# Attention beside a Fourier filter on one core: every fourth part of the maxima takes the bank of the background products

## The chip, the cores and the metric

The kernel runs on one core of a Trainium2 chip. The metric is the device time of one execution in microseconds. A core has engines that run their own instruction streams and wait for one another by semaphores: TensorE (PE; its weight load is PEld), VectorE (DVE), ScalarE (ACT), GpSimd (POOL), and SyncE (SP), which here only issues transfers (DMAs). TensorE writes its products into PSUM, a memory of eight banks per partition; one bank holds 512 float32 values of each of 128 partitions. DVE and ACT read them from there.

## What is computed

Two independent parts, whose results stand side by side in the output:

```python
# A: attention with a compressive memory, 32 heads of 18, four segments of 512 rows
q, k, v = x @ wq, x @ wk, x @ wv            # per head and segment
for s in range(4):
    p = softmax(qs @ ks.T * scale + mask)   # causal inside the segment
    a_dot = p @ vs
    a_mem = (phi(qs) @ M) / (phi(qs) @ z + 1e-6)
    outs.append(g * a_mem + (1 - g) * a_dot)
    M += phi(ks).T @ vs;  z += phi(ks).sum()
a = concat(outs) @ wo
# B: a global filter
b = irfft2(rfft2(x) * (w_r + 1j * w_i))
```

## The kernel before

The program runs in three stretches: the forward transform of B with the projections of A; the inverse transform of B, into which the first steps of the attention are already woven (the prologue); and the attention itself, from about 347 us on, which this text is about. Its order is written out by hand: engines execute their instructions as the Python code emits them.

The attention loop (`attention`) runs over steps `t` from 0 to 132. A step is one head of one segment, 512 queries against 512 keys; four steps make a group `k` and eight steps a stack of eight heads. Segment `g` holds 32 steps. In one step four kinds of work are interleaved on PE:

- `s1(t+11)`, the **maxima**, eleven steps ahead. It computes the scores of a head once, in bf16, only to find the row maxima. Each `part` takes one PSUM bank, fills it with matmuls (line 687), and DVE reduces it with a custom instruction and a read of the accumulator (line 691). An even step of the loop has three parts (384 and 128 columns; 512; two of 256), an odd step two, so four steps have ten.
- `mpath`, once in four steps: the maxima of four heads are copied by POOL (lines 703, 704), transposed by PE into a bank (`mt`, line 707, also tag "s1"), copied by ACT (line 710) and sent by a DMA into two more rows of the queries, so that the next product has the maximum subtracted.
- `s2(t)`, the **scores again**, keys on the partitions, in banks of tag "s2" (lines 723, 727, 728, 733). ACT takes the exponential of each bank into `P` (lines 724, 729, 734), and POOL clears the triangle above the diagonal (line 736).
- `pv`, in every odd step sixteen matmuls of `P` with the values into bank "pv" (line 760); ACT copies the sum out once in four steps (`U`, line 766).

Beside them runs the **background** list `bg`: one piece of a generator is emitted in some of the steps by `run_bg(rate)`. It first holds `late_setup` (loads and casts of the output weights, no PSUM); from step 34 on `den` (denominators of the memory), and, appended by a lane that prepares reciprocals, `mixed` and `oproj` of the segment before (memory products, combination, output projection). Their products take tag "post" through `post(...)`, which turns to tag "s1" from step 117 on.

PSUM in the attention: `s1` has three banks (pool `ps1`), `s2` three, `pv` one and `post` one:

```python
ps1=L1.enter_context(PP(tc,"ps1",dict(s1=3)))
...
tp=pool(es,"tp2",2); ps=es.enter_context(PP(tc,"ps",dict(s2=3,pv=1,post=1)))
```

A tag's banks are taken in turn, so a new tile waits until the reader of the tile that had the bank is done; for `s1` that is the tile three back, where `mt` counts as one.

Of the kernel before, what the change touches and what calls it, by code (L numbers as in the profile page):

```python
# [5 lines left out]
F32=mybir.dt.float32; F32R=mybir.dt.float32r  # L6
# [403 lines left out]
class ATT:  # L410
# [268 lines left out]
    def s1(s,t):  # L679

        nc=s.nc; k,hh=divmod(t,4); n,qd=divmod(k,2); h=4*qd+hh
        Q,K=s.Qs[n%3],s.Ks[n%4]; tp=s.sm
        assert (n,0) in s.loaded and (n,1) in s.loaded,(t,n)
        if hh==0: s.mg[k]=tp.tile([128,4,4],F32,name="mg")
        def part(*J):
            p=s.ps1.tile([128,512],F32,name="s1",tag="s1")
            for o,i,e in J: nc.tensor.matmul(p[:,o:o+128*i+128],Q[:108,h+e,128*i:128*i+128],K[:108,h+e,:128*(i+1)],start=True,stop=True)  # L687
            for o,i,e in J:
                w=128*(i+1); b=max(256,w-128*e)
                junk=tp.tile([128,b],BF,name=f"junk{b}",bufs=1)  # L690
                nc.vector.tensor_tensor_reduce(out=junk[:,:w],in0=p[:,o:o+w],in1=s.mask[:,512-w:],scale=1.0,scalar=-3.0e38,  # L691
                    op0=OP.add,op1=OP.max,accum_out=s.mg[k][:,hh+e,i:i+1])
        part((0,2,0),(384,0,0))
        yield
        part((0,3,0))
        yield
        if hh%2: part((0,1,-1),(256,1,0))
        yield
# [247 lines left out]
    def begin(s,sm,sp,ps1):  # L946
        s.late=[]; s.now=-1
        s.sm,s.sp,s.ps1=sm,sp,ps1
        s.mh=sm.tile([128,8,16],BF,name="mh",bufs=1); s.nc.gpsimd.memset(s.mh,0.0)
        s.mg={};s.P={};s.vs={};s.rc={};s.am={};s.pq={};s.ux={};s.rate=1.2;s.potag=s.rest=None  # L950
    def prologue(s):

        nc,io=s.nc,s.io
        yield
        s.load_v(0)
        q=s.stack_dmas(1,0)+s.stack_dmas(1,1)+s.stack_dmas(2,0)+s.stack_dmas(2,1)+[lambda: s.load_v(1)]+s.stack_dmas(3,1)
        for i in range(2): yield
        i=0
        for t in range(11):
            for _ in s.s1(t):  # L960
                for _ in range(1+(i%24==0)):
                    if q: q.pop(0)()
                i+=1
                yield
            if 2<=t<6: nc.gpsimd.dma_start(s.Ks[t-2][108:110].rearrange("p h c -> p (h c)"),io["neg1"])
            if t in (3,7): m=s.mpath(t//4); next(m)
            if t in (4,8): next(m); next(m,None)
        assert not q
# [3 lines left out]
    def attention(s,tp,ps):  # L972
        nc=s.nc; s.tp,s.ps,s.psm,s.mtag=tp,ps,s.ps1,"s1"
        s.homes()
        def steps(gen,i):
            for _ in range(i):
                try: next(gen)
                except StopIteration: return
        m=None
        q=[]  # L980
        qu=[]
        bg=[s.late_setup(tp)]
        state=dict(acc=0.0)
        def run_bg(rate):
            state["acc"]+=rate
            if state["acc"]>=1:
                state["acc"]-=1
                while bg:
                    try: next(bg[0]); break
                    except StopIteration: bg.pop(0)  # L990
        lane=[]
        for t in range(133):
            k,hh=divmod(t,4); n,qd=divmod(k,2); g=k//8
            if hh==0 and qd==0:
                if 0<n<14: q+=s.stack_dmas(n+2,0)
                if 0<n<13: q+=s.stack_dmas(n+3,1)
                if n+2<16: q.insert(6,lambda n=n: s.load_v(n+2))
            st=t%32
            if t in (18,21,24,27,30): s.pq_load(1,ORD[(18,21,24,27,30).index(t)])
            if t==34: bg.append(s.den(1,lane))  # L1000
            if st==8 and g>0:
                def ln(g=g):
                    r=s.recip(s.rD[g-1],s.rrD[g-1],s.g1,False,"rr",2)
                    for i in range(8):
                        if 2<i<6: s.ux_load(g-1,ORD[i-3])
                        next(r); yield
                    yield from r
                    bg.append(s.mixed(g))
                    o=s.oproj(g-1)
                    if g<3: bg.append(itertools.islice(o,4)); bg.append(s.den(g+1,lane))  # L1010
                    bg.append(o)
                lane.append(ln())
            if t==125: lane.append(s.recip(s.rD[3],s.rrD[3],s.g1,False,"rr"))
            a=s.s1(t+11) if t+11<128 else iter(())
            b=s.s2(t) if t<128 else iter(())
            for _ in range(3 if t%8==0 else 1):
                if q: q.pop(0)()
            if qu: qu.pop(0)()
            steps(a,1)
            steps(b,1)  # L1020
            run_bg(0)
            steps(a,1)
            steps(b,1)
            if 4<=t-1<132: s.pv((t-5)//4,(t-5)%4)
            run_bg(s.rate)
            steps(a,1)
            if hh==1 and m is not None: steps(m,1)
            steps(b,1)
            if hh==1 and m is not None: steps(m,1)
            if hh==0 and k+2<32: m=s.mpath(k+2); next(m)  # L1030
            if hh==0 and s.rest: s.rest(); s.rest=None
            if t>=7 and t%4==3:
                s.pv_out((t-7)//4)
                if t%8==3:
                    u=s.u_dmas((t-11)//8)
                    if t<124: s.later(1,lambda u=u: qu.extend(u))
                    else: qu+=u
            for l in list(lane):
                try: next(l)
                except StopIteration: lane.remove(l)  # L1040
            if qu: qu.pop(0)()
            s.due(t)
        assert not q
        s.potag="s2"; s.last_parts()
        if qu: qu.pop(0)()
        b=s.recip(s.rD[3],s.rrD[0],s.g1,False,"rd"); next(b)
        for u in range(3): s.ux_load(3,u)
        while qu: qu.pop(0)()
        i=0
        while bg or i<10:  # L1050
            for l in list(lane):
                try: next(l)
                except StopIteration: lane.remove(l)
            run_bg(1.0)
            i+=1
            s.due(132+i)
            if i in (3,8,10): s.last_tile((3,8,10).index(i),"rr")
            if i==3: s.ux_load(3,3)
            if i==5: next(b); next(b); next(b)
            if i in (6,7): next(b)  # L1060
            if i==7: s.ux_load(3,4)
        assert not lane
        s.due(999)
        for _ in b: pass
        s.last_low()
        for t in range(3):
            for u in range(7):
                s.last_proj(u,t)
                if t==2 and u==3: s.last_low()
                if t==2 and u in (1,4): s.last_tile(3 if u==1 else 4,"rd")  # L1070
        s.last_low()
        for u in range(7): s.last_proj(u,3)
        o=[s.tp.tile([128,4,512],F32,name=f"P{i}").rearrange("p a b -> p (a b)") for i in range(2)]
        o=[o[tb//3][:,576*(tb%3):576*(tb%3)+576] for tb in range(4)]
        nc=s.nc
        for u in range(8):
            if u==6:
                for t in range(4): s.last_proj(7,t)
            tb,hf=divmod(u,2); s.last_proj(u,4); c=slice(288*hf,288*hf+288) if u>5 else slice(0,576)
            (nc.vector.tensor_copy if hf else nc.scalar.copy)(o[tb][:,288*hf:288*hf+288],s.acc[u])  # L1080
            if hf or u>5: nc.sync.dma_start(s.io["ya"][1536+128*tb:1664+128*tb,c],o[tb][:,c])
# [108 lines left out]
```

## Time and profile before

| | |
|---|---|
| runs shown | 683.86, 684.14, 684.6 us (median 684.14) |
| profiled execution | 683.95 us; span from first to last instruction 682.2 us |
| busy share of the span | PE 98%, weight load 71%, DVE 79%, ACT 64%, POOL 28% |
| granted TensorE clock | 0.999 |
| costliest groups in the attention | maxima on DVE (line 691) 219.6 us, pv on PE (line 760) 82.2 us |

In the profile a row is one instruction or a run of like ones: start, length, engine, line, operation, tiles. A number in brackets at the end of a row is the engine's idle time just before it, and what ended that idle time. "idle" counts only time with no instruction recorded as running; PE's matmuls are pipelined, so the next one may start well before the row of the last one ends.

### The profile page before, as it was taken

How to read it: one execution, taken by the hardware profiler on the slowest of the kernel's cores; microseconds unless marked ns; L12 is line 12 of the kernel's file. 1: busy time of each engine (PE TensorE's matmuls, PEld its weight loads, DVE VectorE, ACT ScalarE, POOL GpSimd, SP SyncE). 2: the span in 40 equal slices, each digit the busy share in tenths (PEclk: the TensorE clock that was granted, in tenths of full speed). 3: DMA queues.
4: the chain of work that ended last, by engine and by line, in shares of the span. 5: the costliest groups of instructions: out<-in, count | busy, mean ns of one | idle time of the engine just before them, and what ended most of it. 6: DMA issues, size and time to landing. Idle time of an engine off the chain costs nothing.

```text
span 682.2 us, 14101 instructions
## 1 busy us (share of the span) xinstructions
PE 669.0 (98%) x4776; PEld 487.0 (71%) x4776; DVE 541.0 (79%) x1509; ACT 433.5 (64%) x900; POOL 193.0 (28%) x392
## 2 busy tenths in 40 slices
PE   9999999999999999999989999999999999999997
PEld 5999779879879879999954444444566445663497
DVE  5998989889789779598778888998766888667543
ACT  4876795585585384544358877777756777656521
POOL 2111000100200102556416433445323663135410
PEclk9999999999999999999999999999999999999999
DMA  9896476596387679699336765776646576423152
GB/s 338 301 311 186 137 198 200 151 300 203 113 240 222 178 211 319 196 284 272 110 121 176 207 185 151 204 205 174 173 139 188 155 186 167 125 87 92 29 170 78
DMA packets 76034, 127.57 MB, mean 187 GB/s; under 512 B 12813, under 2 KB 44203, under 8 KB 72371
## 3 DMA queue, kind: packets, MB, share of 16 engines
q1 hardware_dynamic: 69310, 110.67, 55.7%
q0 software_dynamic: 5632, 15.76, 8.0%
q8 instruction: 37, 0.61, 0.4%
q10 hardware_dynamic: 1020, 0.25, 0.2%
q14 instruction: 35, 0.28, 0.1%
HBM read 81.78 MB, written 43.92 MB: 184 GB/s over the span
## 4 chain that ended last, share of the span: by engine, by line
PE 84%; DVE 5%; DMA 4%; ACT 3%; issue 2%; POOL 1%; SPq 0%; ACTq 0%; DVEq 0%; POOLq 0%
PE pj L487 15%; PE pv L760 11%; PE s L687 11%; PE pjv L487 8%; PE po L908 5%; PE i L331 4%; PE i L320 4%; PE f L145 4%; PE c L166 4%; PE s L723 3%; PE s L727 3%; PE pn L835 2%; PE s L733 2%; PE po L937 2%; PE pm L559 2%
## 5 line engine op out<-in xcount | busy, mean ns | idle before, releaser
L691 DVE CUSTOM_DVE_ANT_0 junk<-s,x 128x384 bf16<-128x384 f32 (+3 forms) x512 | 219.6, 486 | 49.0 <-PE s L687 47.6
L736 POOL TENSOR_SCALAR_AFFINE_SELECT P<-P 128x512 f32<-128x512 f32 (+2 forms) x135 | 80.3, 617 | 61.3 <-ACT P L724 58.0
L760 PE MATMUL pv<-P,vs 128*32 128x512 f32 (+3 forms) x1024 | 82.2, 439 | 0.5 <-POOL P L736 0.4
L724 ACT ACTIVATE P<-s 128x512 f32<-128x512 f32 x128 | 77.3, 604 | 8.3 <-PE s L723 7.1
L729 ACT ACTIVATE P<-s 128x512 f32<-128x512 f32 x128 | 77.0, 602 | 2.8 <-PE s L728 2.7
L734 ACT ACTIVATE P<-s 128x512 f32<-128x512 f32 x64 | 38.3, 598 | 46.3 <-PE s L733 45.4
L687 PE MATMUL s<-Ks,Qs 108*128 108x512 bf16 (+3 forms) x256 | 57.9, 299 | 2.2 <-DVE mg L691 2.0
L760 PEld LDWEIGHTS pv<-P,vs 128*32 128x32 f32 x1024 | 26.8, 109 | 45.5 <-issue 36.3
L487 PE MATMUL pj<-x,wqkh 128*128 128x512 f32 x162 | 56.1, 408 | 0.0
L232 DVE TENSOR_TENSOR Z<-Z 128x580 f32<-128x580 f32 (+2 forms) x51 | 45.9, 913 | 0.6
L691 DVE DVE_READ_ACCUMULATOR2_ANT mg<- 128x1 f32 x512 | 42.5, 83 | 0.0
L548 POOL MEMSET vt<- 128x32 f32 x16 | 2.3, 162 | 139.2 <-PE pm L559 79.2
L320 PE MATMUL i<-civ,Y 128*128 128x256 f32 (+1 forms) x288 | 39.6, 289 | 0.9 <-POOL Y L305 0.9
L687 PEld LDWEIGHTS <-Qs 108*128 108x128 bf16 x320 | 29.5, 97 | 13.0 <-issue 6.2
L320 PEld LDWEIGHTS i<-civ,Y 128*128 128x128 f32 (+1 forms) x288 | 36.8, 181 | 1.9 <-POOL Y L305 1.3
L331 PE MATMUL i<-itab,T 128*128 128x290 f32 (+1 forms) x224 | 36.0, 304 | 0.1
L487 PE MATMUL pj<-x,wqkl 128*128 128x512 f32 x90 | 35.5, 395 | 0.0
L487 PE MATMUL pj<-xh,wqkh 128*128 128x512 f32 x90 | 35.5, 395 | 0.0
L487 PE MATMUL pj<-xh,wqkl 128*128 128x512 f32 x90 | 35.5, 395 | 0.0
L487 PEld LDWEIGHTS pj<-x,wqkh 128*128 128x128 f32 x162 | 30.5, 189 | 6.4
L506 DVE SCALAR_TENSOR_TENSOR ex<-pj,ex 128x512 f32<-128x512 f32 (+1 forms) x28 | 19.3, 689 | 19.4 <-ACT ex L504 19.4
L500 ACT CAST sp<-pj 128x512 bf16<-128x512 f32 x36 | 21.3, 591 | 18.1 <-PE pj L487 14.4
(207 smaller groups left out, 1697.2 us busy)
## 6 DMA issues: line engine op xcount, KB each, us to landing
qkD<-sp SPq DMA_DIRECT2D x32, 384.0 KB
xin<-xb SPq DMA_DIRECT2D x16, 384.0 KB
cfw<-cfw POOLq DMA_DIRECT2D x16, 384.0 KB, 5.1
civ<-civ POOLq DMA_DIRECT2D x16, 384.0 KB, 7.7
Ks<-qkD SPq DMA_DIRECT2D x12, 512.0 KB
x<-qkD SPq DMA_DIRECT2D x10, 512.0 KB
Qs<-qkD SPq DMA_DIRECT2D x10, 512.0 KB
vs<-vD SPq DMA_DIRECT2D x16, 310.5 KB
```

Of the source, the lines that this page charges most:

```text
L232: s.nc.vector.tensor_tensor(o,a,b,op=op)
L320: nc.tensor.matmul(p[:m,k],Y[i][:,q,c*128:c*128+m],cc[:,hl,o:o+256],start=n==0,stop=n==5)
L331: nc.tensor.matmul(p,x,t,start=n==0,stop=n==6)
L487: s.nc.tensor.matmul(out,a,b,start=i==0,stop=i==len(L)-1)
L687: for o,i,e in J: nc.tensor.matmul(p[:,o:o+128*i+128],Q[:108,h+e,128*i:128*i+128],K[:108,h+e,:128*(i+1)],start=True,stop=True)
L691: nc.vector.tensor_tensor_reduce(out=junk[:,:w],in0=p[:,o:o+w],in1=s.mask[:,512-w:],scale=1.0,scalar=-3.0e38, op0=OP.add,op1=OP.max,accum_ ...
L724: nc.scalar.activation(P[0][:,hh],p0,AF.Exp,scale=SC)
L729: nc.scalar.activation(P[1][:,hh],p1,AF.Exp,scale=SC)
L734: nc.scalar.activation(P[2][:,hh-1:hh+1].rearrange("p h c -> p (h c)"),p2,AF.Exp,scale=SC)
L736: nc.gpsimd.affine_select(out=x[:,a:b],in_=x[:,a:b],pattern=[[0,b-a],[1,128]],compare_op=OP.is_ge,fill=0.0,base=0,channel_multiplier=-1)
L760: nc.tensor.matmul(s.pvt[32*hh:32*hh+32,128*j:],vt[:,152*j+19*h:152*j+19*h+32],mv[0][:,hh,mv[1]],start=j==0,stop=j>1,skip_group_check=True)
L908: nc.tensor.matmul(ps,a[t][:r,c],b[:r,t,w],start=i==0,stop=i==13)
```

## The change

A counter `n1` counts the parts of the maxima. While a flag `spare` is set, every fourth part takes its bank from tag "post" instead of "s1". The flag is set at the top of each step: before step 34, and later whenever the background list is empty at that moment. It is not set in the prologue.

```diff
         def part(*J):
-            p=s.ps1.tile([128,512],F32,name="s1",tag="s1")
+            s.n1+=1
+            p=s.ps.tile([128,512],F32,name="s1",tag="post") if s.spare and s.n1%4==0 else s.ps1.tile([128,512],F32,name="s1",tag="s1")
             for o,i,e in J: nc.tensor.matmul(p[:,o:o+128*i+128],Q[:108,h+e,128*i:128*i+128],K[:108,h+e,:128*(i+1)],start=True,stop=True)
...
-        s.mg={};s.P={};s.vs={};s.rc={};s.am={};s.pq={};s.ux={};s.rate=1.2;s.potag=s.rest=None
+        s.mg={};s.P={};s.vs={};s.rc={};s.am={};s.pq={};s.ux={};s.rate=1.2;s.potag=s.rest=None; s.n1=0; s.spare=False
...
         for t in range(133):
+            s.spare=t<34 or not bg
             k,hh=divmod(t,4); n,qd=divmod(k,2); g=k//8
```

The order of the instructions is the same on every engine; what differs is for which semaphore some of them wait. PE in steps 6 and 7 of the loop, before (`s_...` are score banks; those of line 687 are parts of the maxima, those of lines 723 to 728 the second scores):

```order
L687 LDWEIGHTS Qs_3168
L687 MATMUL s_4492<-Ks_3170,Qs_3168 128x512 [waits DVE_49]
L727 LDWEIGHTS x_2634
L727 MATMUL s_4496<-x_2634 128x384 [waits Activation_49]
L728 LDWEIGHTS x_2634
L728 MATMUL s_4496<-x_2634 128x128
L687 LDWEIGHTS Qs_3168 [waits PE_49]
L687 MATMUL s_4502<-Ks_3170,Qs_3168 128x256 [waits Activation_49]
L687 LDWEIGHTS Qs_3168
L687 MATMUL s_4502<-Ks_3170,Qs_3168 128x256
L687 LDWEIGHTS Qs_3168
L687 MATMUL s_4510<-Ks_3170,Qs_3168 128x384 [waits DVE_49]
```

The same place with the change (the lines of the file are one further down):

```order
L688 LDWEIGHTS Qs_3168
L688 MATMUL s_4492<-Ks_3170,Qs_3168 128x512
L728 LDWEIGHTS x_2634
L728 MATMUL s_4496<-x_2634 128x384 [waits Activation_49]
L729 LDWEIGHTS x_2634
L729 MATMUL s_4496<-x_2634 128x128
L688 LDWEIGHTS Qs_3168
L688 MATMUL s_4502<-Ks_3170,Qs_3168 128x256 [waits DVE_49]
L688 LDWEIGHTS Qs_3168
L688 MATMUL s_4502<-Ks_3170,Qs_3168 128x256
L688 LDWEIGHTS Qs_3168 [waits PE_49]
L688 MATMUL s_4510<-Ks_3170,Qs_3168 128x384 [waits Activation_49]
```

Here the 512-column part takes the bank "post" and waits for nothing new; the part of two 256s, which waited for ACT's copy of the transposed maxima, now waits for an earlier reduce of DVE; the wait for ACT stands one part further down. Elsewhere the rows read alike and the awaited count of the semaphore differs.

## The prediction

> **What bounds the kernel now.** I read the page first (busy time, granted clock), then stretches of the attention stage, then the list of waits, then the timeline of single engines. The page:
>
> ```profile
> span 682.2 us, 14101 instructions
> PE 669.0 (98%) x4776; PEld 487.0 (71%) x4776; DVE 541.0 (79%) x1509; ACT 433.5 (64%) x900; POOL 193.0 (28%) x392
> PEclk9999999999999999999999999999999999999999
> ```
>
> TensorE (PE) is marked busy for 98% of the span at the full granted clock. What matters is whether that time is work. The next rows are stretches (us; then busy time of PE, its weight load, VectorE, ScalarE, GpSimd): steps 8 to 33 of the attention loop, all in the part where the change acts; the first steps; and a stretch around steps 42 to 45. The two rows behind them are the whole list of PE's waits from 347 to 414 us (total, times, longest).
>
> ```profile
> 362.68:412.90 50.22, 50.07 (x425) 23.56 (x424) 44.28 (x211) 41.21 (x84) 23.74 (x44) 1.00 0.76 203
> 347.66:358.53 10.87, 9.11 (x66) 4.46 (x65) 10.78 (x50) 8.30 (x16) 2.69 (x8) 1.00 0.39 124
> 429.60:438.14 8.54, 7.38 (x63) 3.33 (x62) 8.51 (x35) 6.89 (x16) 3.47 (x10) 1.00 0.86 223
> ...
> PE s L687 <- DVE mg L691: 0.9, 2, 0.5
> PE mt L707 <- DVE mg L691: 0.7, 1, 0.7
> ```
>
> Read alone, this says that there is next to nothing to win: 50.07 of 50.22 us busy, 1.6 us of waits, and no transfer among them. But a row of PE lasts longer than the work in it. Here is PE in steps 20 to 23 (start, length; the 512-column matmuls are 0.38 us long):
>
> ```profile
> 385.64 0.38 PE L687 MATMUL s<-Ks,x 108*128 108x384 bf16 x2
> 385.87 0.38 PE L723 MATMUL s<-Qs,Ks 110*128 110x512 bf16 x1
> 386.08 0.38 PE L687 MATMUL s<-Ks,x 108*128 108x512 bf16 x1
> 386.30 0.33 PE L727 MATMUL s<-Qs,Ks 110*128 110x384 bf16 x1
> ...
> 386.52 0.38 PE L687 MATMUL s<-Ks,x 108*128 108x256 bf16 x2
> 386.89 0.38 PE L687 MATMUL s<-x,Qs 108*128 108x384 bf16 x2
> 387.11 0.38 PE L723 MATMUL s<-Qs,Ks 110*128 110x512 bf16 x1
> 387.51 0.38 PE L687 MATMUL s<-x,Qs 108*128 108x512 bf16 x1
> 387.72 0.33 PE L727 MATMUL s<-Qs,Ks 110*128 110x384 bf16 x1
> ...
> 389.25 0.23 PE L707 MATMUL mt<-idb,mh 128*128 128x128 bf16 x1
> 389.54 0.38 PE L687 MATMUL s<-x,Qs 108*128 108x384 bf16 x2
> ...
> 390.36 0.22 PE L728 MATMUL s<-Qs,Ks 110*128 110x128 bf16 x1
> 390.58 0.60 PE L687 MATMUL s<-x,Qs 108*128 108x256 bf16 x4
> 391.01 0.38 PE L723 MATMUL s<-Qs,Ks 110*128 110x512 bf16 x1
> 391.40 0.38 PE L687 MATMUL s<-x,Qs 108*128 108x512 bf16 x1
> ```
>
> Undisturbed, the matmul behind one of 512 columns starts 0.21 us later (385.87, 386.08, 386.30), although its row lasts 0.38. So PE can stand still for 0.17 us without any idle time in the list. Name the ten parts of four steps A, B, C (even step), D, E (odd step), F, G, H, I, J; pv and the transpose mt lie between E and F. D starts at 386.89, though the two 256s of C (386.52) took 0.21: lost **0.16**. E starts 0.40 behind the 512 at 387.11: lost **0.19**. H starts at 390.58, 0.05 of work behind 390.36: lost **0.17**. J starts 0.39 behind 391.01: lost **0.18**. A, B, C, F, G, I follow at once. VectorE (DVE) at the same time:
>
> ```profile
> 386.06 0.56 DVE L691 CUSTOM_DVE_ANT_0 junk<-s,x 128x384 bf16<-128x384 f32 x1 [0.46 <-PE s L687]
> 386.55 0.29 DVE L691 CUSTOM_DVE_ANT_0 junk<-s,x 128x128 bf16<-128x128 f32 x1
> 386.76 0.08 DVE L691 DVE_READ_ACCUMULATOR2_ANT mg<- 128x1 f32 x1
> 386.76 0.69 DVE L691 CUSTOM_DVE_ANT_0 junk<-s,x 128x512 bf16<-128x512 f32 x1
> 387.37 0.08 DVE L691 DVE_READ_ACCUMULATOR2_ANT mg<- 128x1 f32 x1
> 388.06 0.09 DVE L691 DVE_READ_ACCUMULATOR2_ANT mg<- 128x1 f32 x1
> 389.96 0.56 DVE L691 CUSTOM_DVE_ANT_0 junk<-s,x 128x384 bf16<-128x384 f32 x1 [0.52 <-PE s L687]
> ```
>
> A's maxima end at 386.84 and B's at 387.45; D starts 0.05 and E 0.06 behind them. That is the ring of three banks: D takes A's bank, E takes B's. J likewise takes G's. H's bank is mt's, which ScalarE (ACT) empties. So PE waits for DVE, and then DVE waits for PE (0.46 and 0.52 in each pair of steps, while PE does pv). The stage is a coupled pair; neither is full.
>
> **The change, part by part.** No instruction is added, removed or moved; the ACT, POOL and SP streams and every DMA stay as they are. Only which earlier reader a part waits for differs. Counting along the loop, 30 of the 320 parts take bank "post": 22 while steps 0 to 33 run, 8 in steps 37 to 49, until the background of the next segment begins. Ten parts per four steps are no multiple of four, so two patterns alternate. X: A, E, I take post, the ring holds B C D mt F G H J. Y: C and G take post, the ring holds A B D E mt F H I J.
>
> *D and E.* D now waits for the J before (X and Y), done long ago. E waits for A in both, ready at 386.84, needed at 387.16 (387.32 less D's 0.16). Both stalls go: 0.35 per first pair. *J* now waits for F: its maxima begin at 389.96 and take, as A's do (386.06 to 386.84), 0.78: 390.74, needed after 391.0. Stall gone: 0.18. *H* in Y waits for E: gone, 0.17. In X H still waits for mt: 0.17 stays. I in Y inherits mt, which is free by the time H started before; nothing. The background's own first matmul in post, in step 34, now comes behind the maxima of a part of step 33, more than a step of work earlier; nothing.
>
> What is late next? ACT and GpSimd rows of the same steps:
>
> ```profile
> 386.80 0.62 ACT L724 ACTIVATE P<-s 128x512 f32<-128x512 f32 x1
> 390.29 0.24 ACT L710 COPY mts<-mt 32x128 bf16<-32x128 bf16 x1
> 388.58 0.22 POOL L704 TENSOR_TENSOR mh<-mg,mh 128x16 bf16<-128x16 f32 x1
> ```
>
> The odd step's L727 (387.72) needs the bank that L724 leaves at 387.42. Moved up by 0.35 it would start at 387.37; with 0.06 for the handover it starts at 387.48: a new wait of 0.11. Behind it on PE stand L728 and pv, and behind pv the next pair's first part, for which DVE waits: the 0.11 is lost in full. A first pair gains **0.24**. mt (389.25) needs L704, over at 388.80, plus 0.06: 0.39 of room, enough. The copy of mt at 390.29 to 390.53 explains H's 390.58. A second pair gains 0.18 (X) or 0.35 (Y).
>
> Can DVE follow? It is busy 44.28 of 50.22 us for 26 steps: 6.81 per four steps, which now take 7.73. After the change they take 7.73 less 0.42 (X) or 0.59 (Y), on average 7.22. Above 6.81, so PE still sets the pace, with 0.4 us of DVE's idle time left.
>
> Two stretches are DVE's, by the window rows above: 10.78 of 10.87 and 8.51 of 8.54 busy. There a bank buys only what lies behind the last reduce.
>
> ```profile
> 357.67 0.22 POOL L704 TENSOR_TENSOR mh<-mg,mh 128x16 bf16<-128x16 f32 x1
> 358.34 0.23 PE L707 MATMUL mt<-idb,mh 128*128 128x128 bf16 x1
> 433.96 0.95 DVE L786 RECIPROCAL ry<-ry 128x128 f32<-128x128 f32 x1
> 435.60 0.38 PE L687 MATMUL s<-Ks,Qs 108*128 108x384 bf16 x2 [1.12 <-DVE mg L691]
> 437.25 0.22 POOL L704 TENSOR_TENSOR mh<-mg,mh 128x16 bf16<-128x16 f32 x1
> 437.95 0.23 PE L707 MATMUL mt<-idb,mh 128*128 128x128 bf16 x1
> ```
>
> At 435.60 PE waits long, behind two reciprocals; but mt at 437.95 can come no earlier than L704 at 437.47 plus 0.06. Of the 1.1 us only **0.38** are to be had. At the start likewise: mt at 358.34 against 357.89 plus 0.06, **0.37** rounded down from 0.39.
>
> The sum. Steps 0 to 7 (X, Y): 0.37, then the second pair of Y 0.35: 0.72. Steps 8 to 31, three X and three Y: 3 x 0.42 + 3 x 0.59 = 3.03. Steps 32, 33: 0.24. Steps 34 to 37: the parts that would gain come from the ring: 0. Steps 38, 39: 0.35. Steps 40 to 47: first pair 0.24; second pair 0.18, which the reciprocals swallow; 0.38; second pair 0.35; so 0.97. Steps 48, 49: 0.24. Together 5.55 us, all on PE, which runs on with no break behind it. From the profiled execution, 683.95 us (span 682.2 and 1.75 around it): 678.4. The median of the runs shown is 684.14, 0.2 above it: **678.6 us**.
>
> Bounds. From above: without the new wait of 0.11 (nine first pairs: 1.0) and with X's H free as well (three: 0.5) the sum is 7.05 us, 677.1. From below: L724 stands behind other ACT work (the copy of U, casts of weights in these steps); if that eats the first pairs' gain altogether (nine times 0.24, 2.2) and the 0.37 and 0.38 with it, 2.6 us are left, 681.5. I take the sum itself, since the rows of ACT that I used already hold a copy of U.
>
> One more thing changes: 13 of the 512-column reduces get a further wait, on DVE's own progress. The 128-column reduces have such a wait now, and the one at 386.55 starts with no idle time behind its neighbour. I take nothing for it; at 0.06 each, the hand-over seen above, it would be 0.8 us, out of DVE's remaining idle time.
>
> **The rivals.** (1) *ScalarE binds earlier*: L724 and L727 hold the odd step, and the first pairs gain nothing: 5.55 less 2.2 is 3.4, 680.7; with the two DVE stretches lost too, 681.5. For it: ACT is busy 41.21 of 50.22 us, so 6.3 per four steps, and the new wait of 0.11 is already of this kind. Against: four steps of 7.2 still leave ACT 0.9 of idle time.
>
> (2) *VectorE has no room at all*, because an end of each reduce does not show in its rows; then PE only waits elsewhere, and the time stays 684.1. Against it: the rows run on without a gap as soon as PE is ahead (386.76, 387.37), and each stop ends with "<-PE". [...]
>
> (3) *Given back downstream*: a transfer that sets its own pace, such as the load of the reciprocals needed at step 51, stops PE later; 684.1 at worst. Against: no DMA stands in the list of waits, and the loads are released by PE's own progress.
>
> (4) *Slower*: maxima read from the post bank cost more, because that bank lies beside pv's and is written meanwhile. Four steps have 0.98 of DVE's idle time (0.46 and 0.52) and 2.5 such parts: from 0.39 us more per part DVE is the bound and the time grows. At double a 0.69 reduce, 2.5 x 0.69 less 0.98 is 0.75 per four steps, twelve times: 9 us, 693. Against: the rows of one shape do not vary with the bank now.
>
> **How the numbers follow.** Forecast 0.70 (677.2 to 680.2); rival 1 0.15; rivals 2 and 3 together 0.07; rival 4 0.04; more than forecast 0.04. The range, 676.9 to 681.6, holds the forecast and most of rival 1. A measurement of this kernel tells about 0.2%, 1.4 us, from no change. Faster: 0.70 + 0.04 + most of rival 1 = 0.88; the same 0.08; slower 0.04.
>
> **What would show it.** In steps 8 to 31, four steps take 7.2 us instead of 7.73, alternating near 7.31 and 7.14; D and E follow at once; H keeps its 0.17 in every second group; DVE's idle times fall from 0.46 and 0.52 to 0.2 to 0.35. From step 52 on, every four steps last as before. Wrong it would be if four steps stay at 7.73, if a wait of 0.3 us stands at L727 or L707, or if a gap with a DMA behind it opens near step 51.

## The result, and the profile after

| | before | with the change |
|---|---|---|
| median of four runs, us | 684.21 (683.86 to 684.6) | 678.91 (678.15 to 679.8) |
| ratio, with its 95% interval | | 0.9923 (0.9906 to 0.9940) |
| profiled execution, us | 683.95, span 682.2 | 679.1, span 677.1 |

The kernel became 5.3 us faster, against a forecast of 678.6 us. The page of the changed kernel, its span and the row of busy times:

```profile
span 677.1 us, 14114 instructions
PE 663.7 (98%) x4776; PEld 486.7 (72%) x4776; DVE 541.0 (80%) x1509; ACT 432.5 (64%) x900; POOL 193.6 (29%) x392
```

PE has the same 4776 matmuls as before and is still marked busy for 98% of the span, yet its busy time is 5.3 us shorter. The stalls that went were inside its rows, as the prediction read them. The 13 further instructions in the count are semaphore waits of DVE (417 in the trace, 404 before): the 13 further waits of the prediction are instructions of their own. The stretches that were shown of before, with their ends at the same instructions (us, then busy PE, its weight load, DVE, ACT, POOL):

```profile
362.40:409.57 47.17, 47.08 (x426) 23.52 (x424) 44.27 (x213) 40.56 (x84) 23.53 (x44) 1.00 0.80 220
348.09:358.56 10.47, 8.49 (x66) 4.43 (x65) 10.38 (x49) 8.07 (x16) 2.30 (x7) 1.00 0.41 128
425.65:433.76 8.11, 7.08 (x63) 3.29 (x62) 8.07 (x34) 6.79 (x16) 3.31 (x9) 1.00 0.95 238
```

Steps 8 to 33 take 47.17 us instead of 50.26 (the prediction's row of 50.22 ends 0.04 before step 34 starts), with DVE's 44.27 us unchanged. The two stretches that DVE fills went from 10.87 to 10.47 and from 8.54 to 8.11. And the list of PE's waits from 347 to 410 us:

```profile
PE mt L708 <- DVE mg L692: 1.3, 2, 1.1
PE s L724 <- ACT P L725: 0.4, 1, 0.4
PE s L728 <- DVE yout L339: 0.3, 1, 0.3
```

The two waits for a bank of the maxima have left the list; what is left lies in steps 0 to 7, and stands at the transposes and at the second scores. By the letter, the prediction's sign of being wrong, a wait of 0.3 us at L727 or L707 (one line further down now), is there: 1.15 us before the first transpose and 0.30 before one of the second scores. But VectorE sets the pace in those steps (busy for 10.38 of 10.47 us in the second row of stretches), and 1.27 us stood at the same place before, 0.55 at the maxima and 0.72 at the transpose. From step 8 to step 41 the list is empty. PE in steps 20 to 23 of the changed kernel, a group of the kind that the prediction called Y:

```profile
384.23 0.38 PE L724 MATMUL s<-Qs,Ks 110*128 110x512 bf16 x1
...
384.89 0.38 PE L688 MATMUL s<-Ks,x 108*128 108x256 bf16 x2
385.11 0.38 PE L688 MATMUL s<-x,Qs 108*128 108x384 bf16 x2
385.33 0.38 PE L724 MATMUL s<-Qs,Ks 110*128 110x512 bf16 x1
385.55 0.38 PE L688 MATMUL s<-x,Qs 108*128 108x512 bf16 x1
385.83 0.32 PE L728 MATMUL s<-Qs,Ks 110*128 110x384 bf16 x1
```

D (385.11) and E (385.55) follow 0.22 us behind their neighbours, where they stood still for 0.16 and 0.19 before. The next row starts 0.29 behind E (by the unrounded times) instead of 0.22: the new wait, 0.07 us. What it waits for is in ACT's timeline of the same place:

```profile
384.70 0.58 ACT L767 COPY U<-pv 128x512 f32<-128x512 f32 x1
385.17 0.61 ACT L725 ACTIVATE P<-s 128x512 f32<-128x512 f32 x1
```

The exponential of L725 ends at 385.78, and L728 starts 0.05 behind it. In front of the exponential ACT copies `U`. On DVE, the maxima of 512 and of 384 columns in steps 8 to 31, grouped (count, busy us, mean ns, idle time before them and its releaser); first before, then with the change:

```profile
L691 DVE CUSTOM_DVE_ANT_0 junk<-s,x 128x512 bf16<-128x512 f32 x24 | 16.5, 686 | 0.0
L691 DVE CUSTOM_DVE_ANT_0 junk<-s,x 128x384 bf16<-128x384 f32 x24 | 13.3, 556 | 5.4 <-PE s L687 5.4
```

```profile
L692 DVE CUSTOM_DVE_ANT_0 junk<-s,x 128x512 bf16<-128x512 f32 x24 | 16.5, 686 | 0.0
L692 DVE CUSTOM_DVE_ANT_0 junk<-s,x 128x384 bf16<-128x384 f32 x24 | 13.3, 555 | 2.6 <-PE s L688 2.2
```

A reduce is as long as it was, also when it reads bank "post" (686 ns before and after). DVE's idle time went from 5.4 to 2.6 us in 24 steps, in single stops of 0 to 0.36 us where 0.2 to 0.35 was forecast.

Where the 5.12 us between the two spans came from, taken from the start of line 723 (724 with the change) in each step of the two profiled executions:

| part of the loop, us | before | after | gained |
|---|---|---|---|
| start of the loop | 347.64 | 348.07 | -0.43 |
| steps 0 to 7 | 15.04 | 14.33 | 0.71 |
| steps 8 to 31 | 46.37 | 43.53 | 2.84 |
| steps 32, 33 | 3.89 | 3.64 | 0.25 |
| steps 34 to 37 | 8.73 | 8.73 | 0.00 |
| steps 38, 39 | 3.83 | 3.51 | 0.32 |
| steps 40 to 47 | 16.79 | 15.78 | 1.01 |
| steps 48, 49 | 3.89 | 3.64 | 0.25 |
| steps 50 to 126 | 192.17 | 192.49 | -0.32 |
| the rest | 43.88 | 43.40 | 0.48 |

Steps 0 to 49, the only ones whose banks differ, gained 5.38 us. The other three rows come to -0.27. Their instructions are the same in both kernels. An unchanged kernel in another execution (e10_rr_alone, below) started its loop at 347.83 and had 44.13 us in the last row, but 98.54 us in steps 0 to 49 against 98.55. So a few tenths of a microsecond in the first and last rows are no effect of the change, while 0.05 us in steps 0 to 49 can be read. Of the 0.32 lost in steps 50 to 126, 0.25 lies in steps 90 to 93, which took 8.96 us in each of the other ten profiled executions; what came in there is open.

### The profile page after: what moved, and what is told of

It is laid out like the page before. It is cut to its first block, busy times and chain, and to the rows that moved or that the text cites. A ratio compares the mean times of both kernels' runs of the same rounds, so it can differ in the third digit from the quotient of the medians.

```text
span 677.1 us, 14114 instructions
## 1 busy us (share of the span) xinstructions
PE 663.7 (98%) x4776; PEld 486.7 (72%) x4776; DVE 541.0 (80%) x1509; ACT 432.5 (64%) x900; POOL 193.6 (29%) x392
## 4 chain that ended last, share of the span: by engine, by line
PE 83%; DVE 5%; ACT 5%; DMA 3%; issue 2%; POOL 2%; ACTq 0%; POOLq 0%; SPq 0%; DVEq 0%
PE pj L487 15%; PE pv L761 10%; PE s L688 9%; PE pjv L487 8%; PE po L909 7%; PE i L331 4%; PE i L320 4%; PE f L145 4%; PE c L166 4%; PE s L724 3%; DVE junk L692 3%; PE s L728 2%; PE po L938 2%; PE pn L836 2%; PE s L734 2%
## 5 line engine op out<-in xcount | busy, mean ns | idle before, releaser
L725 ACT ACTIVATE P<-s 128x512 f32<-128x512 f32 x128 | 77.2, 603 | 8.1 <-PE s L724 6.0
```

Of the source, the lines that this page charges most:

```text
L725: nc.scalar.activation(P[0][:,hh],p0,AF.Exp,scale=SC)
```

## The experiments

**The theory** is the prediction's: a part of the maxima waits for the earlier reader of its own bank, PE stands still when that reader is late, and the further bank lets each part wait for one that is long done. PE still sets the pace, and VectorE follows. **The rivals** that were left: what matters is merely one bank more, wherever it goes; or VectorE, ScalarE or a transfer takes over as soon as PE is ahead. In the tables steps are timed as above, and "groups" are four steps of 8 to 31, in order; before, all six took 7.73 us, with the change 7.31, 7.15, 7.37, 7.15, 7.40 and 7.15.

### Every fifth part

Ten parts per four steps are twice five, so the same two parts, C and H, always take "post".

```diff
-            p=... if s.spare and s.n1%4==0 else ...
+            p=... if s.spare and s.n1%5==0 else ...
```

> Every fifth part takes the bank post: always C and H, 24 or so parts instead of 30. Theory (what counts is which earlier reader a part waits for): the ring holds A B D E mt F G I J, so D, E, H and J all lose their wait in every group, and each group is like pattern Y: 7.15 us per four steps, steps 8 to 31 take 42.9 us against 43.5 with every fourth part and 46.4 before; H's 0.17 to 0.23 at its L688 row is gone. Time 0.6 to 0.9 us under the changed kernel, 678.1. Rival (the gain goes with the number of parts that get the further bank): four fifths of 5.3 us, 680.0, and 44.1 us for steps 8 to 31.

Measured: 678.91 us, ratio 0.9927 (0.9914 to 0.9940). Steps 8 to 31 took 43.00 us, the groups 7.15, 7.15, 7.16, 7.15, 7.24 and 7.15. So the third stall of group X, H behind the copy of `mt`, went as it should once H is never behind `mt`. The rival is refuted here: fewer parts take the further bank, and these steps took 43.00 us, not 44.1. But the whole was no faster than the change, since steps 34 to 37 took 9.49 us instead of 8.73. PE's timeline there, and the list of its waits from 404 to 425 us, both of this kernel:

```profile
413.67 0.60 PE L688 MATMUL s<-Ks,Qs 108*128 108x256 bf16 x4 [0.70 <-ACT ds L816]
```

```profile
PE s L688 <- ACT ds L816: 0.7, 1, 0.7
```

In step 34 the flag is set at the top, when the list of background work is still empty, and a few lines later `den` is put on it. H took "post" behind den's own product and waited until ACT had copied that out. In the change as given no fourth part falls on that step, which is luck of the count.

### Every second part

```diff
-            p=... if s.spare and s.n1%4==0 else ...
+            p=... if s.spare and s.n1%2==0 else ...
```

> Every second part takes the bank post: A, C, E, G, I. Theory (a part waits for the last reader of its bank): E cannot start before the maxima of C are done, 2.5 us behind A's start, 0.69 later than before; I not before those of G, 0.61 later than before. Four steps take about 9.0 us instead of 7.73, steps 8 to 31 54 us instead of 46.4; the time rises to 695 to 698. Rival (a further bank helps by the number of parts that use it): 678 or less.

Measured: 696.50 us, ratio 1.0182 (1.0167 to 1.0196). Each group took 8.86 us, steps 0 to 49 110.79 instead of 98.55. PE and DVE of this kernel in one pair of steps:

```profile
373.00 0.38 PE L688 MATMUL s<-Ks,Qs 108*128 108x256 bf16 x2 [0.21 <-DVE mg L692]
374.30 0.38 PE L688 MATMUL s<-Ks,x 108*128 108x512 bf16 x1 [0.48 <-DVE mg L692]
```

```profile
372.17 0.56 DVE L692 CUSTOM_DVE_ANT_0 junk<-s,x 128x384 bf16<-128x384 f32 x1 [0.90 <-PE s L688]
...
374.17 0.08 DVE L692 DVE_READ_ACCUMULATOR2_ANT mg<- 128x1 f32 x1
...
376.75 0.56 DVE L692 CUSTOM_DVE_ANT_0 junk<-s,x 128x384 bf16<-128x384 f32 x1 [1.21 <-PE s L688]
```

C's last accumulator read ends at 374.25 and E, which takes the same single bank, starts at 374.30. A ring of one for every second part is tighter than a ring of three for all, though no bank fewer is in use than in the change. That refutes "one bank more, wherever it goes". The row of PE's idle time and the time from one reduce to the next show the coupled pair again: VectorE is idle for 0.90 and 1.21 us, because PE waits for VectorE. In the kernel before, the stall of 0.33 us in every first pair (D 0.15, E 0.18) was of this kind, and the further bank took it away; the 8.86 us show that the count of banks alone does not decide.

### Only before step 34

```diff
-            s.spare=t<34 or not bg
+            s.spare=t<34
```

> The flag is set before step 34 only. Theory (the gain is local and nothing downstream takes or adds any): steps 0 to 33 as in the changed kernel, steps 37 to 49 as before, 24.5 us; gain 3.8 of the 5.3 us: 680.4. Rival (the gain of the first part is given back downstream, or the second part's gain rests on the first): 678.9 or 684.2.

Measured: 680.69 us, ratio 0.9947 (0.9935 to 0.9959). Steps 8 to 31 took 43.53 us as with the change, and steps 38 to 49 as before (3.83, 7.73, 9.05, 3.89); steps 0 to 49 together 94.74, of the change's 5.38 us 3.81. The gains are local and add up, so nothing that happens after step 34 takes back what came before.

### The copy of U later

`U` is copied behind the first exponential of the next step instead of ahead of it, until step 50, and its transfers go one step later.

```diff
+        lane=[]; uq=[]
...
             steps(b,1)
+            while uq: uq.pop(0)()
...
-                s.pv_out((t-7)//4)
+                if t<50: uq.append(lambda k=(t-7)//4: s.pv_out(k))
+                else: s.pv_out((t-7)//4)
...
-                    if t<124: s.later(1,lambda u=u: qu.extend(u))
+                    if t<124: s.later(2 if t<50 else 1,lambda u=u: qu.extend(u))
```

On top of the change:

> As the changed kernel, but up to step 50 the copy of U stands on ScalarE behind the first exponential of the next step instead of ahead of it (its transfers one step later). Theory: the new wait at L727/L728 of the first pairs is the first exponential held up by the copy of U; it goes, 0.08 to 0.11 us per four steps, about 1 us in all: 678.0. Rival (ScalarE is late for its whole load, or that wait has another cause): L728's wait stays or moves to L734, and the time is the changed kernel's, 678.9, or 0.3 to 1 us more if pv then waits for the copy.

Measured: 678.40 us, ratio 0.9918 (0.9904 to 0.9931). The groups took 7.24, 7.08, 7.38, 8.08, 7.44 and 7.08. Three of the six, the first two and the last, are 0.07 us shorter than with the change, which is the new wait: it stood behind the copy of `U`. In the group of step 16, H waited 0.31 us behind `mt` instead of 0.23, and nothing was left of it. And one group lost 0.93. ACT and PE of this kernel there, and the list of PE's waits from 386 to 396 us:

```profile
391.38 0.62 ACTq L714 DMA_DIRECT2D x<-mts  x1
392.04 0.60 ACT L725 ACTIVATE P<-s 128x512 f32<-128x512 f32 x1 [2.04 <-PE s L688]
```

```profile
392.69 0.38 PE L724 MATMUL s<-x,Ks 110*128 110x512 bf16 x1 [0.81 <-ACT P L725]
```

```profile
PE s L724 <- ACT P L725: 0.8, 1, 0.8
```

ACT issues the transfer of the maxima rows itself (L714). Here it issued it only at 391.38 and stood still for 2.04 us, with an exponential queued behind it. The bracket names PE, but the scores had long been written. In the record of the semaphores ACT waits, just ahead of this transfer, for the semaphore on which an unrelated load, that of the values, reports its landing; the last part landed at 391.30, and ACT's wait ended at 391.34. The same wait stands in all eleven traces. In before, too, the transfer follows that landing by 0.08 us. In e2 the load took 7.0 us from issue to landing instead of at most 5.7 in the others. Why it took longer is open, and no run took the wait away.

In steps 50 to 53 e2 lost 0.36 us more (8.73 us instead of 8.37), most of it in one wait of PE:

```profile
446.07 0.38 PE L885 MATMUL pb<-rr,sel 96*72 96x512 bf16 x1 [0.32 <-DMA rr<-rrD]
```

The same wait is larger in e8 below. The profiled execution of e2, 680.35 us, was the slowest of its five, and its steps 0 to 49 took 93.72 us against 93.17 with the change, so these losses need not be in the other four. The 678.40 can't be told from the change's 678.91.

The same edit without the change:

> The kernel before, with no part in the bank post, and only the copy of U moved behind the first exponential up to step 50. Theory (without the further bank PE comes to L727 after that exponential is done, so nothing waits for it): four steps stay at 7.73 us, time 684.2. Rival (the copy of U is a limit of its own): 0.07 to 0.1 us less per four steps, 683.2.

Measured: 684.34 us, ratio 1.0003 (0.9992 to 1.0014), all six groups 7.73. In the kernel before, the copy of `U` held nobody up. The wait at L728 is made by the change.

### Every fifth part, and step 34 left out

```diff
-            p=... if s.spare and s.n1%4==0 else ...
+            p=... if s.spare and s.n1%5==0 else ...
...
-            s.spare=t<34 or not bg
+            s.spare=t<34 or t>34 and not bg
```

> As with every fifth part (C and H), but step 34 is left out, where H had to wait 0.76 us for ScalarE to empty the bank of the background's den product. Theory (that wait alone made steps 34 to 37 longer, 9.49 us instead of 8.73): they are back at 8.73, steps 8 to 31 stay at 43.0, steps 0 to 49 take 92.6 us against 93.2 with every fourth part; time 678.2. Rival (the fifth part's order costs there for another reason): 9.5 us again, 678.9.

Measured: 678.06 us, ratio 0.9916 (0.9899 to 0.9933). Steps 34 to 37 took 8.73 us again, steps 0 to 49 92.62, as expected, against 93.17 with the change. Steps 8 to 31, as a stretch of before and of this kernel:

```profile
362.68:409.05 46.37, 46.23 (x392) 21.78 (x391) 40.91 (x195) 38.19 (x79) 22.41 (x40) 1.00 0.76 203
```

```profile
362.33:405.32 42.99, 42.97 (x392) 21.57 (x391) 40.82 (x197) 37.36 (x79) 22.33 (x40) 1.00 0.83 223
```

VectorE's work is the same, 40.9 and 40.8 us, and its share went from 88 to 95%. As long as VectorE's rows stay as they are, its time is the floor for what further banks could give: the stretch stood 5.5 us above it before, and stands 2.2 above it now.

### Both, and what it meets behind

The copy of `U` later, with every fifth part and step 34 left out:

> The kernel of the run e7_fifth_clear with the copy of U behind the first exponential up to step 50. Theory: another 0.07 us per four steps, as in the undisturbed groups of e2_u_later (7.08 against 7.15), 0.8 us in all if no transfer is late: steps 8 to 31 take 42.5 us, time 677.5. Rival (a transfer that ScalarE issues waits for the landing of the values' load, as in the one group of 8.08 us of e2_u_later, and the tighter loop meets it regularly): one or more groups 0.3 to 1 us longer, 678.2 or more.

Measured: 678.94 us, ratio 0.9917 (0.9901 to 0.9934). Steps 0 to 49 took 92.16 us, the least so far (groups 7.08, 7.08, 7.17, 7.11, 7.21, 7.08). Steps 8 to 31 came to 42.74 us where 42.5 was expected, and no group was 0.3 us longer, so the rival with the values' load did not show. But steps 50 to 126 took 194.11 instead of 192.19. PE's timeline and the list of its waits from 430 to 455 us:

```profile
445.20 0.38 PE L885 MATMUL pb<-rr,sel 96*72 96x512 bf16 x1 [1.92 <-DMA rr<-rrD]
```

```profile
PE pb L885 <- DMA rr<-rrD: 1.9, 1, 1.9
```

This is the place that the prediction's third rival named: the reciprocals (`rr`) that the first background product needs in step 51 come by a transfer, it now ends last, and 1.9 us are given back. But it does not set a pace of its own. Its issue moves with PE: it came 5.44 us ahead of PE's need in the kernel before, 5.18 with the change and 5.13 here (438.15, against 443.28, where the wait begins). What changed is the time from issue to landing: 7.0 us here and 5.4 in e2, which have both the further bank and the later copy of `U`, and 4.5 to 5.0 in the eight executions that lack one of the two or both. To see whether the wait is this load alone, the reciprocals of the first segment were written and loaded one step earlier, on top of e8:

```diff
-                    r=s.recip(s.rD[g-1],s.rrD[g-1],s.g1,False,"rr",2)
+                    r=s.recip(s.rD[g-1],s.rrD[g-1],s.g1,False,"rr",2-(g==1))
...
                     bg.append(s.mixed(g))
+                    if g==1: yield
```

> The kernel of the run e8_clear_u, with the first segment's reciprocals written and loaded one step earlier, so that their load stands on SP's queue ahead of the query and key loads of step 48 and not behind them. Theory (in e8_clear_u PE's 1.9 us at L885 are that load alone, landing late behind 0.9 MB of queries): the wait is gone, steps 50 to 127 take 192.2 us again instead of 194.1, steps 0 to 50 stay at 92.2; time 677.2 or a little less. Rival (the transfers are late whatever their order): a wait of 0.5 us or more stays at L885, 678 or more.

Measured: 678.20 us, ratio 0.9907 (0.9893 to 0.9921). The queue of SP in e8 has the load behind the next stack's queries:

```profile
436.30 0.53 SPq L665 DMA_DIRECT2D Qs<-qkD  x1
438.15 0.31 SPq L799 DMA_DIRECT2D rr<-rrD  x1
```

In this kernel it stands ahead of them:

```profile
437.37 0.53 SPq L799 DMA_DIRECT2D rr<-rrD  x1
438.00 0.53 SPq L665 DMA_DIRECT2D Qs<-qkD  x1
```

The load landed 2.3 us after its issue. The wait at L885 is gone and steps 50 to 126 took 192.20 us; steps 0 to 49 stayed at 92.14. That shows that the 1.9 us were this load alone. The time did not follow: the median is 678.20, where 677.2 was expected. The profiled execution, 679.25 us, was the slowest of the five. In it, what came from the start of step 127 on took 45.22 us instead of 43.33, though PE's last instruction came only 0.17 later. The difference lies in what ends the program behind PE, where SP waited 2.9 us for the landing of the output instead of 1.2. Why is open.

The kernel before once more, with no line changed (the label, e10_rr_alone, names a move of the reciprocals, which is not in it):

> The kernel before once more, unchanged, for the repeatability of its profile: four steps take 7.73 us, steps 0 to 50 98.55 us within 0.05.

Measured in one run: 684.63 us, steps 0 to 49 98.54 and 50 to 126 192.17, as before to 0.01 us. What the earlier reciprocals do without the change was not run.

By the medians, e7 (678.06), e9 (678.20) and the change (678.91) can't be told apart, since their intervals overlap. By the trace of steps 0 to 49 they can: 92.62, 92.14 and 93.17 us.

## Why the prediction was right

It was right in the time and in the way: the changed place gained 5.38 us where the sum had 5.55, and the experiments show the mechanism. That the sizes came so close is in part luck. By its steps:

- **The reading of PE's rows.** D, E and J lose their stalls, and H its own in every group Y. Steps 8 to 31 show it; the groups Y took 7.15 us where 7.14 was forecast. Two small errors cancel in that: undisturbed starts are 0.22 us apart and not 0.21, so the four stalls come to 0.66 us (D 0.15, E 0.18, H 0.17, J 0.16) and not 0.70, and the new wait is 0.07 us and not 0.11.
- **The groups X were mis-sized**, the only term that was off by more than 0.05 us: 3 x 0.42 forecast, 0.42, 0.36 and 0.33 measured, so 2.84 instead of 3.03 in these steps. "In X H still waits for mt: 0.17 stays" holds in two of them. In the group of step 16 a cast of weights stood in front of ACT's copy of `mt`, and H waited 0.23. In the group of step 24 the transpose itself came 0.09 late, behind POOL's L705:

```profile
393.80 0.55 DVE L692 CUSTOM_DVE_ANT_0 junk<-s,x 128x384 bf16<-128x384 f32 x1
```

```profile
394.32 0.22 POOL L705 TENSOR_TENSOR mh<-mg,mh 128x16 bf16<-128x16 f32 x1
```

```profile
394.60 0.23 PE L708 MATMUL mt<-idb,mh 128*128 128x128 bf16 x1
```

  The 384-column reduce in front of that chain has no idle time before it: VectorE was behind, after three short instructions of its own on lines 634 to 636 (389.37 to 389.91), and the transpose starts 0.06 after L705 (394.54). The "0.39 of room" at the transpose was read from one group of before; with PE ahead, it was 0.13 in most groups and nothing in this one. The same group is the longest of e1 and e7 too (7.24), with H out of the way.
- **The new wait at the odd step** was forecast at 0.11 and measured at 0.07. With the copy of `U` out of its way it went, as e2 shows; without the change it isn't there, as e6 shows.
- **Where VectorE limits.** 0.37 and 0.38 were forecast for the two stretches, 0.40 and 0.43 measured (10.87 to 10.47, 8.54 to 8.11).
- **Steps 40 to 47.** 0.97 forecast, 1.01 measured. The second pair's 0.18 that the reciprocals swallow is first won in steps 42 and 43 (that group gained 0.42) and then lost in the next, which gained 0.59 where 0.38 and 0.35 would make 0.73.
- **Steps 34 to 37** gained nothing, as forecast. That rested on which parts are fourth parts: e1 put one there and lost 0.76 us.
- **The rivals.** *ScalarE binds earlier*: only the 0.07. *VectorE has no room*: refuted, its idle time was halved and its share reached 95% in e7. The kernel before showed the room already: the next reduce starts 0.61 us after the start of one of 0.69 (386.76 and 387.37). *Dearer reads from "post"*: refuted, 686 ns before and after, and no cost of the 13 further waits can be seen. *Given back downstream*: did not happen with the change. The reciprocals landed 0.96 us before PE needed them in the kernel before, 0.46 in the same kernel once more (e10) and 0.33 with the change (from the semaphore record and the row of L885), so two executions of one kernel differ by almost as much as the two kernels do. The prediction's argument against this rival, that the loads are released by PE's own progress, holds in the traces (issued 5.44, 5.18 and 5.13 us ahead of PE's need in before, the change and e8). What it did not have is that such a load can take 7.0 us instead of 4.5 to 5.0, as in e8. The writes of `U`, which the later copy puts shortly ahead of that load, stand there in e6 too, where it took 4.6 us; what made it longer is open.

## What to carry to other kernels

A matmul row is here longer than the time to the next matmul (0.38 us against 0.22 at 512 columns), so stalls of about the difference (0.15 to 0.18 us each, 5.4 us in 50 steps) stand in no list of waits; compare the distance from start to start with that of undisturbed neighbours. When a ring of banks holds up an engine, ask for each tile which earlier reader it waits for, not how many banks there are: a fourth bank taken by every fourth or fifth tile brought four steps from 7.73 us down to 7.15 to 7.40, and the same bank taken by every second tile brought them up to 8.86. And before an engine is moved ahead, read in more than one execution how far ahead of their use the transfers land: 0.3 to 1.0 us were left here, and one load that took 2 us longer cost PE 1.9 us.

## What the runs showed of the hardware

- **The clock.** In one of the eleven profiled executions, that of e1_fifth, the granted TensorE clock fell to half in the midst of the program for 3.4 us (3.30 of it in the second row of stretches), in the inverse transform, far from any edit. PE's rows just before, then the stretches around it (the last columns are granted clock, DMA share and GB/s):

```profile
278.92 0.76 PE L320 MATMUL i<-civ,Y 128*128 128x256 f32 x4 [0.47 <-ACT Y L304]
280.33 0.39 PE L320 MATMUL i<-civ,Y 128*128 128x256 f32 x1 [0.65 <-POOL Y L305]
280.99 2.41 PE L320 MATMUL i<-civ,Y 128*128 128x256 f32 x13 [0.27 <-POOL Y L305]
```

```profile
275.00:282.00 7.00, 5.61 (x43) 5.01 (x42) 2.70 (x5) 3.97 (x10) 3.12 (x7) 0.99 0.44 122
282.00:285.30 3.30, 3.30 (x16) 3.30 (x15) 1.12 (x2) 1.90 (x5) 3.12 (x5) 0.50 0.71 171
285.30:290.00 4.70, 4.70 (x39) 4.55 (x38) 2.70 (x6) 2.27 (x6) 1.69 (x3) 1.00 0.85 241
```

  Its loop began at 349.98 us, some 2 us later than the others (346.95 to 348.58); half of 3.4 us is at most 1.7 of that. This is why its span of 678.9 is not set against theirs and steps are compared instead. In the 3.4 us before the fall PE was busy for 2.06 us and idle in pieces of at most 0.65; what made the clock fall is open.
- **A transfer issued by a computing engine** stopped that engine for 2.04 us in e2, by the semaphore record because the issue waits for the landing of another transfer (landed at 391.30, issued at 391.38), and cost PE 0.93 us.
- **The issue of a small load** (96 KB) ahead of larger ones (the first 512 KB) in SP's queue, 0.8 us earlier by the two traces, was worth 1.9 us: in e8 the small load of `rr`, issued at 438.15 behind the queries, took 7.0 us to land and held PE until 445.20; issued at 437.37 and ahead of them in e9 it took 2.3 us and held nobody. Order and time were not told apart.
